# Two of the eight heads of the second group's convolution on GpSimd, in an eight-head convolution and token/channel mixer

## The chip, the cores and the metric

The kernel runs on one core of one Trainium2 chip. The metric is the device time of one execution in microseconds (us); of the kernel before there are three runs, and their median counts. "PE" is TensorE's matmul row in the profile, "PEld" its weight loads, "DVE" VectorE, "ACT" ScalarE, "POOL" GpSimd, "SP" the engine that only issues DMAs here.

## The reference

The input `x` has 8 batches of 4096 tokens with 192 channels. A causal convolution of 7 taps runs over the tokens, with one set of softmax weights for each of 8 heads of 24 channels. Its result `x` goes through a mix over the tokens and a mix over the channels, each two products with a maximum between them, added to what went in.

```python
w = softmax(weight, axis=-1)                       # 8 heads x 7 taps
x_unf = x_pad[:, idx, :].reshape(B, S, K, H, group)
x = np.einsum('hk,bskhg->bshg', w, x_unf)          # the convolution
xt = x.transpose(0, 2, 1)
h = np.maximum(xt @ w_tok1, 0.0) @ w_tok2          # token mix, 4096 -> 256 -> 4096
u = x + h.transpose(0, 2, 1)
h2 = np.maximum(u @ w_ch1, 0.0) @ w_ch2            # channel mix, 192 -> 1536 -> 192
return (u + h2).astype(np.float32)
```

## The kernel before

**Groups.** The batches are worked in five groups: batch 0, batch 1, then three pairs. For each group a *first stage* makes the convolution and the first token product (`stage1`, sums in `ps_a`, result `h1`). Then the group goes tile by tile (8 tiles of 512 tokens a batch) through the second token product (`mix2`), the transposes (`transposed`, result `own`), the first channel product (`channel1`, results `hh` and `hl`) and the second (`channel2`, result `osb`), and is stored. Products that need more than TensorE's reduced fp32 are split in a high and a low part: `hh`/`hl`, `own[0]`/`own[1]`, `t2s` and so on. ScalarE copies the high part out of PSUM (L973, L896), VectorE forms the low part as the difference (L974, L897).

**What runs beside what.** The first stage of group i+1 is worked in the background of the tiles of group i. For this change the stretch that matters is group 0's tiles, behind which three things run: the decoding of `w_tok2` (VectorE lines L172, L173, L176, L179 and L186 on 128x512 pieces, into `t2s`), the storing of its decoded pieces (ScalarE L1111 into `stage`, then a DMA of SP's queue), and the first stage of group 1, which is batch 1 alone (`nb == 1`). Groups 2 to 4 have two batches (`nb == 2`), and group 0's convolution is made on TensorE.

**The convolution of group 1.** It goes in four rounds (`q2` = 0 to 3) of 1024 tokens. For each round two halves of the input are loaded (`raw0` with heads 0 to 3, `raw1` with heads 4 to 7, one buffer each), with 8 tokens and 6 more of halo in each of 128 partitions. For each head, tap 0 is a scaled copy on ScalarE (L631) into the result `xc`, and taps 1 to 6 are six `scalar_tensor_tensor` instructions on VectorE (L633) that add weight times `raw` to `xc`, in place, on 128x192 elements. Heads go in pairs (`taps` runs heads h and h+1), so a call is two instructions of one tap. When a round is done, `store` sends `xc` to DRAM by a DMA of GpSimd's queue (L657), and 16 small matmuls per round (L721) add the round to `ps_a`. `xc` has two buffers in turn (`xc0`, `xc1`).

**The planner.** `Background` holds the background work as streams of items, each with a cost in VectorE's time. After each piece of a tile, `fg` adds that piece's TensorE and VectorE time to two running sums, and `fill` then takes items for as long as VectorE's sum is behind TensorE's (`if self.dve >= self.pe + until`). So the program order of all engines is set when the kernel is built, from these costs, and every engine works its own list in that order. A tap's item costs `2 * (RB * nb * G / 0.96 + 130)` ns, 660 for group 1. Among the streams the one goes first that has done the smallest share of its own total.

**GpSimd before** makes some set-up, two copies `u<-xc` of 128x768 (L912), small memsets (L623) and issues the stores `out_dram<-osb` (L1020) and `xcd<-xc` (L657) in program order, each waiting for its data at the head of the queue.

Of the kernel before, what the change touches and what calls it, by code (L numbers as in the profile page):

```python
# [8 lines left out]
F32 = mybir.dt.float32  # L9
# [3 lines left out]
ALU = mybir.AluOpType  # L13
# [101 lines left out]
def conv_mixer_kernel(ctx: ExitStack, tc: tile.TileContext, x, weight, w_tok1, w_tok2, w_ch1, w_ch2, out):  # L115
    nc = tc.nc
    B, S, D = x.shape
    H, K = weight.shape
    G = D // H
    JT = w_tok1.shape[1]  # L120
    FF = w_ch1.shape[1]
    P = 128
# [11 lines left out]
    RB = 8  # L134
# [20 lines left out]
    cw = const.tile([P, H, K], F32, name="cw")  # L155
# [442 lines left out]
    def stage1(gi, pools):  # L598
        bs = GROUPS[gi]
        nb = len(bs)  # L600
# [9 lines left out]
        HH, DH = H // 2, D // 2  # L610

        def load(q2, part):
# [10 lines left out]
                    nc.gpsimd.memset(raw[0:1, 0:HALO, i, :], 0.0)  # L623
            return raw

        def conv(raw, xc, h, k):
            rawm = raw.rearrange("p r b d -> p (r b) d")
            src = rawm[:, k * nb:(k + RB) * nb, h % HH * G:(h % HH + 1) * G]
            dst = xc[:, :, h * G:(h + 1) * G]
            if k == 0:  # L630
                nc.scalar.activation(out=dst, in_=src, func=AF.Copy, scale=cw[:, h, 0:1])  # L631
            else:
                nc.vector.scalar_tensor_tensor(  # L633
                    out=dst, in0=src, scalar=cw[:, h, k:k + 1], in1=dst, op0=ALU.mult, op1=ALU.add
                )
# [4 lines left out]
        def mark(*key):  # L640
            done[key] = max(bg.pe, bg.dve)

        def begin(q2, part):
            states[q2]["raw", part] = load(q2, part)
            mark("load", q2, part)

        def taps(q2, h, k):
            st = states[q2]
            if k == 0 and h == 0:
                st["xc"] = pools(q2 % 2).tile([P, RB * nb, D], F32, name=f"xc{q2 % 2}")  # L650
            for i in range(2):
                conv(st["raw", h // HH], st["xc"], h + i, k)

        def store(q2):
            xc = states[q2]["xc"].rearrange("p (j b) d -> p j b d", b=nb)
# [76 lines left out]
        def loaded(q2, part):  # L732
            at = done.get(("load", q2, part))
            return None if at is None or pools(q2 % 2) is None else at + (2e3 + 2e3 * nb if q2 else 10e3)

        def tap(q2, h, k):
            it = Item(lambda: taps(q2, h, k), cost=2 * (RB * nb * G / 0.96 + 130) if k else 0)
            if h % HH == 0 and k == 0:
                it.lag = 100

                def gate():
                    if h == 0 and q2 > 1 and ("split" if nb > 1 else "mixed", q2 - 2, last_q) not in done:
                        return None
                    return loaded(q2, h // HH)

                it.gate = gate
            convolving.append(it)
# [33 lines left out]
        for q2 in range(NS):  # L781

            tap(q2, 0, 0)
            for h in range(0, H, 2):
                for k in range(1, K):
                    if k == K // 2 and (h + 2) % HH:
                        tap(q2, h + 2, 0)
                    tap(q2, h, k)
                if h + 2 == HH:
                    tap(q2, HH, 0)  # L790
                if h % HH == HH - 2 and q2 + 1 < NS:
                    convolving.append(Item(lambda q2=q2, h=h: begin(q2 + 1, h // HH), lag=600))
            convolving.append(Item(lambda q2=q2: store(q2)))
            for q in range(0, last_q + 1, 2):

                for k in range(2):
                    prepare(q2, q + k)
                for k in range(2):
                    multiply(q2, q + k)
# [260 lines left out]
    def first_items():  # L1060
# [31 lines left out]
        def through():  # L1092

            decode_ctx.close()
            conv_pool(0)
            starts[2] = stage1(2, lambda k: cps[k])
# [28 lines left out]
    for gi, bs in enumerate(GROUPS):  # L1125
        nb = len(bs)
# [12 lines left out]
        for q in range(NT):  # L1139
            nxt = (gi, q + 1) if q + 1 < NT else (gi + 1, 0)  # L1140
            for i, b in enumerate(bs):
# [12 lines left out]
                if ahead:  # L1154
                    h = channel1(abc[i])
# [67 lines left out]
```

## Time and profile before

| | |
|---|---|
| median of 3 runs | 2064.75 us (2064.7 to 2065.62) |
| profiled execution, its own time | 2066.69 us |
| its span in the trace | 2064.8 us, granted TensorE clock 0.999 |
| busy: PE, PEld | 2052.5 us (99%), 1902.8 us (92%) |
| busy: DVE, ACT, POOL | 1404.0 us (68%), 760.2 us (37%), 101.7 us (5%) |
| chain that ended last | PE 90%, DVE 6%, DMA 2%, ACT 1% |

A line such as `L633 DVE ... x192 | 68.4, 412` gives a group of instructions: 192 of them were busy 68.4 us together, 412 ns each; instructions of one engine overlap at their ends, so that the sum over a group can be less than count times mean, and the distance between two starts ("pitch") is less than a duration. In the timeline a row has the start and the length of a run of like instructions and, in brackets, how long the engine had been idle before it and for whom. In a table of windows each engine has its busy time and its count of instructions.

### The profile page before, as it was taken

How to read it: one execution, taken by the hardware profiler on the slowest of the kernel's cores; microseconds unless marked ns; L12 is line 12 of the kernel's file. 1: busy time of each engine (PE TensorE's matmuls, PEld its weight loads, DVE VectorE, ACT ScalarE, POOL GpSimd, SP SyncE). 2: the span in 40 equal slices, each digit the busy share in tenths (PEclk: the TensorE clock that was granted, in tenths of full speed). 3: DMA queues.
4: the chain of work that ended last, by engine and by line, in shares of the span. 5: the costliest groups of instructions: out<-in, count | busy, mean ns of one | idle time of the engine just before them, and what ended most of it. 6: DMA issues, size and time to landing. Idle time of an engine off the chain costs nothing.

```text
span 2064.8 us, 41285 instructions
## 1 busy us (share of the span) xinstructions
PE 2052.5 (99%) x17723; PEld 1902.8 (92%) x17723; DVE 1404.0 (68%) x2781; ACT 760.2 (37%) x1305; POOL 101.7 (5%) x167
## 2 busy tenths in 40 slices
PE   9999999999999999999999999999999999999999
PEld 9889999998989989999999999999999999999998
DVE  8899979999559988448965778444445444444444
ACT  4656544434333333224323433233223232233222
POOL 0100000000000000000000000000000000000000
PEclk9999999999999999999999999999999999999999
DMA  9855436554354564232543433322211212222210
GB/s 308 291 154 183 138 120 197 180 164 137 132 160 136 177 170 132 78 103 74 151 124 90 129 122 108 98 60 67 67 45 52 65 50 67 59 67 67 67 32 17
DMA packets 259654, 239.44 MB, mean 116 GB/s; under 512 B 202832, under 2 KB 213584, under 8 KB 257936
## 3 DMA queue, kind: packets, MB, share of 16 engines
q1 hardware_dynamic: 243616, 158.55, 26.6%
q0 software_dynamic: 15856, 78.26, 11.8%
q8 instruction: 140, 2.29, 0.4%
q14 instruction: 42, 0.34, 0.1%
HBM read 146.60 MB, written 71.30 MB: 106 GB/s over the span
## 4 chain that ended last, share of the span: by engine, by line
PE 90%; DVE 6%; DMA 2%; ACT 1%; issue 1%; SPq 0%; POOL 0%; ACTq 0%; POOLq 0%
PE ps_x L934 35%; PE ps_x L1008 16%; PE ps_x L991 16%; PE ps_x L1009 7%; DVE xc L633 2%; PE ps_x L894 2%; PE ps_x L864 2%; PE ps_a L725 2%; PE ps_x L866 2%; PE ps_a L726 2%; PE ps_a L727 2%; PE ps_x L865 2%; DVE hl L974 1%; PE ps_a L426 1%; DMA t2d<-stage 1%; DMA dec_raw<-in_moe_w_tok_dram 1%
## 5 line engine op out<-in xcount | busy, mean ns | idle before, releaser
L973 ACT ACTIVATE hh<-ps_x 128x512 fp32r<-128x512 f32 x756 | 411.1, 597 | 807.2 <-PE ps_x L934 807.1
L974 DVE SCALAR_TENSOR_TENSOR hl<-ps_x,hh 128x512 fp32r<-128x512 f32 x756 | 485.1, 685 | 218.2 <-ACT hh L973 217.7
L934 PE MATMUL ps_x<-own,w_hi 64*128 64x512 f32 x2880 | 607.6, 390 | 1.4 <-DVE hl L974 1.2
L1008 PE MATMUL ps_x<-w,hh 128*128 128x384 f32 x1872 | 542.6, 361 | 0.7 <-DVE hl L974 0.6
L934 PEld LDWEIGHTS ps_x<-own,w_hi 64*128 64x128 f32 x2880 | 429.4, 184 | 55.9 <-issue 6.5
L1009 PE MATMUL ps_x<-w,hl 128*128 128x192 f32 x1872 | 468.8, 250 | 0.0
L934 PE MATMUL ps_x<-other,w_hi 64*128 64x512 f32 x1728 | 450.9, 389 | 0.5 <-DVE osb L1013 0.3
L633 DVE SCALAR_TENSOR_TENSOR xc<-raw,cw,xc 128x384 f32<-128x384 f32 (+1 forms) x768 | 388.7, 561 | 9.2 <-ACT xc L631 9.2
L1009 PEld LDWEIGHTS ps_x<-w,hl 128*128 128x128 f32 x1872 | 357.5, 191 | 0.0
L1008 PEld LDWEIGHTS ps_x<-w,hh 128*128 128x128 f32 x1872 | 351.4, 188 | 1.5 <-DVE hl L974 1.5
L934 PEld LDWEIGHTS ps_x<-other,w_hi 64*128 64x128 f32 x1728 | 314.0, 184 | 33.9 <-DVE hl L974 1.8
L991 PE MATMUL ps_x<-w,hh 64*128 64x384 f32 x2304 | 329.9, 355 | 0.0
L934 PE MATMUL ps_x<-own,w_lo 64*128 64x512 f32 x1440 | 326.5, 387 | 0.0
L991 PE MATMUL ps_x<-w,hl 64*128 64x192 f32 x2304 | 292.2, 247 | 0.1
L934 PE MATMUL ps_x<-other,w_lo 64*128 64x512 f32 x864 | 242.1, 386 | 0.0
L934 PEld LDWEIGHTS ps_x<-own,w_lo 64*128 64x128 f32 x1440 | 218.1, 184 | 24.4
L991 PEld LDWEIGHTS ps_x<-w,hl 64*128 64x128 f32 x2304 | 223.4, 188 | 1.7 <-DVE hl L974 0.8
L991 PEld LDWEIGHTS ps_x<-w,hh 64*128 64x128 f32 x2304 | 219.5, 184 | 0.9
L1012 DVE TENSOR_TENSOR osb<-ps_x,u 128x192 f32<-128x192 f32 x156 | 55.4, 355 | 205.1 <-PE ps_x L1009 204.9
L934 PEld LDWEIGHTS ps_x<-other,w_lo 64*128 64x128 f32 x864 | 159.0, 184 | 16.7
L896 ACT CAST own<-ps_x 128x512 fp32r<-128x512 f32 x120 | 63.4, 595 | 268.7 <-PE ps_x L894 268.5
L999 DVE TENSOR_TENSOR osb<-ps_x,osb 128x192 f32<-128x192 f32 x288 | 103.0, 358 | 17.0 <-DVE osb L999 0.5
(135 smaller groups left out, 1880.4 us busy)
## 6 DMA issues: line engine op xcount, KB each, us to landing
raw<-in_x_dram SPq DMA_DIRECT2D x56, 672.0 KB, 7.4
t<-t2d SPq DMA_DIRECT2D x64, 512.0 KB, 5.0
out_dram<-osb POOLq DMA_DIRECT2D x63, 384.0 KB, 4.3
u<-xcd SPq DMA_DIRECT2D x62, 384.0 KB, 5.6
xcd<-xc POOLq DMA_DIRECT2D x28, 768.0 KB, 7.4
other<-own POOLq DMA_DIRECT2D x24, 768.0 KB, 5.4
t<-t1p SPq DMA_DIRECT2D x32, 512.0 KB, 4.1
t2d<-stage SPq DMA_DIRECT2D x16, 512.0 KB, 4.3
```

Source lines behind the costliest of these rows:

```text
L633: nc.vector.scalar_tensor_tensor(out=dst, in0=src, scalar=cw[:, h, k:k + 1], in1=dst, op0=ALU.mult, op1=ALU.add)
L725: nc.tensor.matmul(out=ps, lhsT=wh, rhs=xh, start=a, stop=False)
L726: nc.tensor.matmul(out=ps, lhsT=wh, rhs=xl, start=False, stop=False)
L896: nc.scalar.copy(out=own[:, 0, c], in_=ps)
L934: nc.tensor.matmul(out=ps, lhsT=w1[w][rows, c, p * P:(p + 1) * P], rhs=t[h][rows, v, c], start=n == 0, stop=n == len(prods) - 1,)
L973: nc.scalar.activation(out=h["hh", f], in_=ps, func=AF.Relu)
L974: nc.vector.scalar_tensor_tensor(out=h["hl", f], in0=ps, scalar=0.0, in1=f32(h["hh", f]), op0=ALU.max, op1=ALU.subtract)
L991: nc.tensor.matmul(out=ps[:, :m], lhsT=h[part, f][ks, ts], rhs=w2[ks, f, :m], start=n == 0 and part == "hh", stop=z and part == "hl",)
L999: nc.vector.tensor_tensor(out=osb[:, j], in0=v, in1=osb[:, j], op=ALU.add)
L1008: nc.tensor.matmul(out=ps[:, :2 * D], lhsT=h["hh", f][:, ts], rhs=w2[:, f, :], start=n == 0, stop=False)
L1009: nc.tensor.matmul(out=ps[:, :D], lhsT=h["hl", f][:, ts], rhs=w2[:, f, :D], start=False, stop=z)
L1012: nc.vector.tensor_tensor(out=rows(osb[:, j]), in0=rows(ps[:, :D]), in1=tokens(u, i)[:, j], op=ALU.add)
```

## The change

A new function `conv_aside` forms a whole head on GpSimd: for tap 0 a `tensor_scalar` product straight into `xc`, and for each of the taps 1 to 6 a product into a small tile `prod` (128x192) and a `tensor_tensor` sum of `prod` and `xc` into `xc`: 13 instructions for a head. It is used where `nb == 1`, which is group 1, for heads 3 and 7 (`h % HH == HH - 1`), all of it at the place in the program where tap 0 of that pair was. VectorE's and ScalarE's instructions of these heads are gone: in four rounds 48 on VectorE and 8 on ScalarE, and 104 are added on GpSimd. The planner's cost of a tap of such a pair is halved.

```diff
+        def conv_aside(pool, raw, xc, h):
+            dst = xc[:, :, h * G:(h + 1) * G]
+            prod = pool.tile([P, RB, G], F32, name="prod")
+            for k in range(K):
+                src = raw[:, k:k + RB, 0, h % HH * G:(h % HH + 1) * G]
+                nc.gpsimd.tensor_scalar(
+                    out=prod if k else dst, in0=src, scalar1=cw[:, h, k:k + 1], scalar2=None, op0=ALU.mult
+                )
+                if k:
+                    nc.gpsimd.tensor_tensor(out=dst, in0=prod, in1=dst, op=ALU.add)
+
+        def aside(h):
+            return nb == 1 and h % HH == HH - 1
+
         def taps(q2, h, k):
...
             for i in range(2):
-                conv(st["raw", h // HH], st["xc"], h + i, k)
+                if not aside(h + i):
+                    conv(st["raw", h // HH], st["xc"], h + i, k)
+                elif k == 0:
+                    conv_aside(pools(q2 % 2), st["raw", h // HH], st["xc"], h + i)
...
-            it = Item(lambda: taps(q2, h, k), cost=2 * (RB * nb * G / 0.96 + 130) if k else 0)
+            it = Item(lambda: taps(q2, h, k), cost=(2 - aside(h + 1)) * (RB * nb * G / 0.96 + 130) if k else 0)
```

**On GpSimd**, from the two memsets of `raw` on: the order of the program before and of the changed one. `osb` is a finished tile of group 0, `xc_897` and the next `xc` are rounds 0 and 1 of the convolution, `raw_765` and `raw_768` the two halves of round 0's input.

```order
L623 MEMSET raw_765 1x576
L623 MEMSET raw_768 1x576
L1020 DMA out_dram<-osb 128x4x192 x2
L657 DMA xcd_76<-xc_897 128x1536
L1020 DMA out_dram<-osb 128x4x192
L657 DMA xcd_76<-xc_1507 128x1536
```

```order
L1038 DMA out_dram<-osb 128x4x192
L631 TENSOR_SCALAR xc_897<-raw_765,cw 128x8x24
L631 TENSOR_SCALAR prod<-raw_765,cw 128x192
L635 TENSOR_TENSOR xc_897<-prod,xc_897 128x8x24
...
L631 TENSOR_SCALAR xc_897<-raw_768,cw 128x8x24
...
L1038 DMA out_dram<-osb 128x4x192
L675 DMA xcd_76<-xc_897 128x1536
L631 TENSOR_SCALAR xc_1439<-raw_1211,cw 128x8x24
```

Between two stores of `xc` there stands now one block of 26 instructions, the 13 of head 3 and the 13 of head 7 of one round, and it stands behind the store of the round before and the store of a tile. (Lines behind the new function are higher by up to 18: L633 is L644 now, L974 is L992, L1020 is L1038.)

**On VectorE**, at the first channel product of the second of the tiles that have convolution behind them (`hl` are the low parts that it gives, `dec_top` and `t2s` the decoding): before, round 0 is still being finished there; now round 1 is.

```order
L974 SCALAR_TENSOR_TENSOR hl_1321<-ps_x,hh_1320 128x512 x2
L172 TENSOR_SCALAR dec_top<-dec_top 128x512
L974 SCALAR_TENSOR_TENSOR hl_1321<-ps_x,hh_1320 128x512 x2
L186 TENSOR_TENSOR t2s<-dec_top,t2s 128x512
L974 SCALAR_TENSOR_TENSOR hl_1323<-ps_x,hh_1322 128x512 x2
L633 SCALAR_TENSOR_TENSOR xc_897<-raw_768,cw,xc_897 128x8x24 x2
L974 SCALAR_TENSOR_TENSOR hl_1323<-ps_x,hh_1322 128x512 x2
L633 SCALAR_TENSOR_TENSOR xc_897<-raw_768,cw,xc_897 128x8x24 x2
```

```order
L992 SCALAR_TENSOR_TENSOR hl_1350<-ps_x,hh_1349 128x512 x2
L179 SCALAR_TENSOR_TENSOR dec_top<-dec_raw,dec_top 128x512
L992 SCALAR_TENSOR_TENSOR hl_1350<-ps_x,hh_1349 128x512 x2
L644 SCALAR_TENSOR_TENSOR xc_1439<-raw_1211,cw,xc_1439 128x8x24 x2
L992 SCALAR_TENSOR_TENSOR hl_1352<-ps_x,hh_1351 128x512 x2
L644 SCALAR_TENSOR_TENSOR xc_1439<-raw_1211,cw,xc_1439 128x8x24 x2
L992 SCALAR_TENSOR_TENSOR hl_1352<-ps_x,hh_1351 128x512 x2
L644 SCALAR_TENSOR_TENSOR xc_1439<-raw_1211,cw,xc_1439 128x8x24 x4
```

The room between the same pairs of `hl` is filled as densely as before, with work that used to come later. Counted in the two orders, from the first `hl` of one tile to the first of the next:

| tile | taps (L633) and decoding steps before | after |
|---|---|---|
| T1 | 34 and 10 | 26 and 14 |
| T2 | 42 and 14 | 36 and 16 |
| T3 | 42 and 14 | 36 and 15 |
| T4 | 46 and 12 | 36 and 6 |
| T5 | 18 and 1 | none, and 24 taps of group 2 |
| T6 | 24 taps of group 2 | none |

On TensorE the last 16 small matmuls of the convolution's rounds (L721) were all in T5; 8 of them are in T4 now and 8 in T5.

## The prediction

> **What bounds the kernel now.** I read the page first. TensorE has a matmul in flight for 99% of the span, VectorE is busy for 68%, and VectorE's load lies in the first fifth of the slices:
>
> ```profile
> PE 2052.5 (99%) x17723; PEld 1902.8 (92%) x17723; DVE 1404.0 (68%) x2781; ACT 760.2 (37%) x1305; POOL 101.7 (5%) x167
> DVE  8899979999559988448965778444445444444444
> ```
>
> So the kernel runs at TensorE's pace, and VectorE can matter only where it is full too. The change touches group 1's convolution. The view of the tile `raw` up to 260 us (count, shortest/median/longest in ns, first and last start) puts its taps behind tiles T1 to T5 of group 0:
>
> ```profile
> L633 DVE SCALAR_TENSOR_TENSOR xc<-raw,cw,xc x189: 406/411/421, 99.9 to 259.7; 128x192 f32<-128x192 f32 x189
> ```
>
> I therefore asked for the table of windows with one window for each tile, from the first channel product (L934) of one to that of the next: T1 to T5, and T6 for comparison. The columns are window, length, then busy time and count of PE, PEld, DVE, ACT, POOL, the granted clock and the DMA share:
>
> ```profile
> 99.62:131.73 32.11, 31.16 (x234) 28.26 (x234) 31.53 (x79) 21.22 (x38) 0.75 (x1) 1.00 0.45 145
> 131.73:167.03 35.30, 35.30 (x265) 33.47 (x264) 34.62 (x87) 22.78 (x39) 1.31 (x2) 1.00 0.65 196
> 167.03:202.93 35.90, 35.88 (x265) 32.72 (x265) 35.59 (x90) 19.85 (x37) 1.31 (x2) 1.00 0.50 147
> 202.93:240.06 37.13, 35.84 (x267) 34.25 (x266) 35.26 (x89) 19.14 (x36) 1.31 (x2) 1.00 0.57 184
> 240.06:275.21 35.15, 35.15 (x267) 33.75 (x266) 25.04 (x62) 19.25 (x30) 1.88 (x3) 1.00 0.45 144
> 275.21:305.13 29.92, 29.92 (x234) 28.85 (x234) 26.61 (x55) 11.87 (x25) 1.28 (x2) 1.00 0.20 63
> ```
>
> T6 and T5 show TensorE's own pace with VectorE slack (26.61 of 29.92, 25.04 of 35.15): 29.92 us for a tile without the convolution's matmuls (L721), 35.15 with 16 of them, so 5.23 for the 16. T1 has none, T2 to T4 have 16 each. Against that pace T1 is 2.19 us long, T2 0.15, T3 0.75, T4 1.98: together 5.07 us, 0.25% of the kernel. In T1 to T3 VectorE is idle for only 0.58, 0.68 and 0.31 us. So **VectorE and TensorE are level there**: taking work from VectorE can win 5 us at the very most, and each microsecond put on it beyond a small room is paid in full. TensorE's waits between 95 and 245 us name VectorE (total, times, longest):
>
> ```profile
> PE ps_x L934 <- DVE hl L974: 0.8, 1, 0.8
> PEld ps_x L934 <- DVE hl L974: 2.0, 3, 1.3
> ```
>
> A difference of 0.2%, 4.1 us, is about what a measurement of this kernel can tell from none.
>
> **What VectorE is relieved of.** A tap's pitch is read from a run of four and the next row (first column start, second length):
>
> ```profile
> 120.68 1.39 DVE L633 SCALAR_TENSOR_TENSOR xc<-raw,cw,xc 128x192 f32<-128x192 f32 x4
> 122.00 0.68 DVE L179 SCALAR_TENSOR_TENSOR dec_top<-dec_raw,dec_top 128x512 uint32<-128x512 uint32 x1
> ```
>
> 1.32 us for four is 0.33 each, and 48 of them are 15.8 us. ScalarE loses eight first taps; it is busy for 21 of 32 us in T1 and I count that at nothing. But the planner knows that the taps got cheaper and fills the room again. With the counts of the two orders (a tap 0.33, a decoding step 0.5 us on average by the rows below) VectorE's list becomes shorter by 0.7 us in T1 (8 taps less, 4 steps more), 1.0 in T2, 1.5 in T3, 6.3 in T4; the remaining 6.4 us are in T5, which already had 10 us idle. So where VectorE is the limit only 3.2 of the 15.8 us arrive.
>
> **What GpSimd's instructions take.** No row shows a product or a sum on GpSimd. The nearest are two memsets, which read nothing, and a copy with one input:
>
> ```profile
> L397 POOL MEMSET corner<- 128x1024 f32 x1 | 0.9, 946 | 0.0
> L408 POOL MEMSET x<- 128x192 f32 x1 | 0.3, 253 | 0.0
> 24.04 0.82 POOL L912 COPY u<-xc 128x768 f32<-128x768 f32 x1 [19.74 <-ACT xc L505]
> ```
>
> The memsets give (946 - 253) / 832 = 0.83 ns an element. The copy is then 0.64 us of elements and 0.18 fixed, and a product on 192 elements 0.16 + 0.18 = 0.34 us; its bounds are 0.25 (the memset of this size) and 0.82 (the copy of four times the size). A sum reads two streams: 0.32 + 0.18 = 0.50 if they take turns, with 0.34 and again 0.82 as bounds. I take 0.34 and 0.50, the scaled copy being the nearest kind. A block of two heads is 14 x 0.34 + 12 x 0.50 = 10.8 us, the four are 43 us, on an engine that was busy for less than 2 us in each tile above. By itself that hides.
>
> The Trainium skill, "GPSIMD Engine Reference", section "3.1 Elementwise — side-by-side cycle accounting", gives about 2.6 cycles an element at 1.2 GHz for a two-input operation, and its section 4.1 advises VectorE for elementwise work for this reason; an estimate from it is 0.42 us of elements for 192, so 0.60 with the fixed 0.18; the four blocks would be 48 us, a tenth more than mine, and the sum at the end +7 instead of +6.
>
> **What they cost VectorE.** GpSimd's two copies are the only rows where it reads SBUF beside a busy VectorE, and both show a blockade. The first rows are the first copy's neighbour and the same instruction undisturbed, then the second copy, its two neighbours, and the like of the last undisturbed:
>
> ```profile
> 24.09 1.32 DVE L172 TENSOR_SCALAR t<-t 128x1024 f32<-128x1024 f32 x1
> 20.48 0.69 DVE L172 TENSOR_SCALAR t<-t 128x1024 f32<-128x1024 f32 x1 [1.24 <-ACT t L170]
> 57.14 1.33 POOL L912 COPY u<-xc 128x768 f32<-128x768 f32 x1 [32.28 <-PE ps_x L859]
> 57.71 0.35 DVE L871 TENSOR_TENSOR u<-ps_x,u 128x192 f32<-128x192 f32 x1
> 57.97 1.31 DVE L176 SCALAR_TENSOR_TENSOR dec_top<-dec_raw,dec_top 128x768 uint32<-128x768 uint32 x1
> 71.86 0.96 DVE L176 SCALAR_TENSOR_TENSOR w2f<-dec_raw,w2f 128x768 uint32<-128x768 uint32 x1
> ```
>
> The L172 issued at 24.09, inside the copy of 24.04 to 24.86, took 1.32 instead of 0.69 us: it ended at 25.41, so it began in effect at 24.72, 0.14 us before the copy's recorded end. The second copy took 1.33 instead of 0.82, behind a VectorE instruction already running, and L176 at 57.97 took 1.31 instead of 0.96. The L871 between them, which reads PSUM and one SBUF tile, took its usual 0.35. So an instruction with two SBUF inputs, or the `tensor_scalar` L172, does not run at the same time as GpSimd's reading ones; one with a PSUM input does. The tap L633 reads `raw` and `xc`, both in SBUF: it is of the blocked kind. The Trainium skill, "SBUF — State Buffer", section "Who interferes with whom", states this as an exclusive lock on a port pair that VectorE's two-port modes and two-SBUF-input operations share with GpSimd, whoever starts first holding it to its end; the trace agrees (0.69 became 1.32), and it speaks against this change.
>
> How much of VectorE's time is of that kind is read from its groups between 95 and 275 us and the window's total:
>
> ```profile
> 95.00:275.00 180.00, 177.74 (x1317) 166.77 (x1316) 165.44 (x409) 104.32 (x181) 6.39 (x10) 1.00 0.52 164
> L633 DVE SCALAR_TENSOR_TENSOR xc<-raw,cw,xc 128x192 f32<-128x192 f32 x192 | 68.4, 412 | 1.0 <-ACT xc L631 1.0
> L974 DVE SCALAR_TENSOR_TENSOR hl<-ps_x,hh 128x512 fp32r<-128x512 f32 x60 | 38.5, 683 | 1.6 <-ACT hh L973 1.4
> L176 DVE SCALAR_TENSOR_TENSOR dec_top<-dec_raw,dec_top 128x512 uint32<-128x512 uint32 x12 | 8.3, 688 | 0.2
> L179 DVE SCALAR_TENSOR_TENSOR dec_top<-dec_raw,dec_top 128x512 uint32<-128x512 uint32 x12 | 8.2, 684 | 0.0
> L186 DVE TENSOR_TENSOR t2s<-dec_top,t2s 128x512 fp32r<-128x512 f32 x12 | 8.2, 684 | 0.0
> L173 DVE TENSOR_SCALAR dec_top<-dec_top 128x512 uint32<-128x512 uint32 x12 | 5.1, 427 | 0.0
> L172 DVE TENSOR_SCALAR dec_top<-dec_top 128x512 f32<-128x512 f32 x12 | 5.0, 419 | 0.4 <-ACT dec_top L170 0.4
> ```
>
> Decoding is 34.8 us in 60 steps, 0.58 each by duration and some 0.5 by pitch (the L179 further up lasts 0.68 and is 0.60 ahead of its follower). After the change the taps are 68.4 x 144/192 = 51.3, so blocked kinds are 86 of 165.4 - 17.1 = 148 us, 58%. GpSimd's blocks start behind a tile's store, so at a first channel product, where `hl` (PSUM input) takes more than half of VectorE's time; I take 50%. The share of GpSimd's 43 us, less 0.14 for each of 104 instructions at their end, is 0.5 x (43 - 15) = 14 us; where both engines have the next instruction ready they take turns, which puts more of GpSimd's work beside blocked kinds, up to 0.5 x 43 = 22. I take **18 us, 4.5 a block**. Bounds: all 104 at 0.25 give 0.5 x 104 x 0.11 = 6 us (1.5 a block), nothing if it never meets; products 0.5 and sums 0.82 give 0.5 x 67 = 34 us (8.5 a block).
>
> **The sum.** T1 to T3 have one block each: VectorE's list grows by 4.5 - 0.7 = 3.8, 3.5 and 3.0 us, together 10.3. From it go the 1.6 us in which VectorE was idle there, and 2 us of lag that six PSUM buffers let pass (an estimate: the planner counts 2.04 us of L934 to fill a pair, and the longest wait of 1.3 above says that there is hardly more). TensorE pays 6.7. T4 has 35.26 - 6.3 + 4.5 = 33.5 us of VectorE work against 35.15 + 2.6 of TensorE's, since half of T5's small matmuls move into it; VectorE is no limit there any more. T4 and T5 were 72.28 and are 70.3 at TensorE's pace. Of the 2.0 us between, 1.3 was a hole whose chain goes back to the DMA of `stage`, which may stay:
>
> ```profile
> 201.89 12.46 DMA t2d<-stage x2
> 210.00:220.00 10.00, 8.71 (x69) 7.75 (x66) 8.44 (x18) 7.68 (x13) 0.00 (x0) 1.00 0.66 231
> ```
>
> I count -1.0. The net is +5.7. The profiled execution takes 2066.69 with a span of 2064.8; the runs' median is 2064.75, and a difference made on the span goes onto that: **2070.5 us**. Later groups have the same items (group 2's first taps move one tile up, into T5's free room), and TensorE at its pace: nothing.
>
> **Rivals.** *It relieves* (0.24): GpSimd's instructions mostly meet `hl` and other PSUM readers, or hold their inputs far more briefly than recorded, so VectorE nets a gain. Against it are both copies, each with a blockade; for it, the blocks' place at the first channel product. At 1.5 us a block T1 to T3 come to -3.2 + 4.5, about their old pace, and T4 and T5 give 1 to 2 back: 2063; with no blockade at all T1 to T3 lose up to 3 of their 3.1 us, so 2060.5. *GpSimd's sums are slow* (0.14): at 1 us for a sum and 0.6 for a product a block is 20.4 us, half of it blocks, 10 a block; T1 to T3 pay 30 - 3.2 - 3.6 = 23.2, T4's list of 39.0 us exceeds TensorE's 37.8 by 1.2 and T4 and T5 together then give back 0.8: 2087. From 8.8 us a block on T4 is short too. *GpSimd is late* (0.04): round n's small matmuls wait for its heads. A block starts when the last round's store is issued; the stores stand some 41 us apart:
>
> ```profile
> 144.16 0.55 POOL L657 DMA_DIRECT2D xcd<-xc  x1 [8.86 <-DVE xc L633]
> 184.61 0.55 POOL L657 DMA_DIRECT2D xcd<-xc  x1 [13.17 <-DVE u L876]
> ```
>
> So a block of 26 must exceed 1.5 us an instruction to be late; at 1.65 it is 3 us late, in four rounds 12 us, 2077. That the planner's new order doesn't relieve VectorE (the change not doing what it says) is already in the sum.
>
> **How the numbers follow.** My case, blocking of 3 to 8 us a block (0.58), runs from about +1 (3 x 3 - 3.2 - 3.6 = +2.2, less 1.0) to +16 (24 - 3.2 - 3.6, less 1.0). Of it I put 0.20 within 4.1 us and 0.38 above; of the relieving case 0.16 within and 0.08 faster; both other rivals are slower. Sums: faster 0.08, same 0.36, slower 0.56. The range 2061.5 to 2083 leaves out the best of the relieving case and the slow sums.
>
> **What would show it.** In the profile after: L644 with a mean above 412 ns and a maximum near 0.9 us, in the four blocks only, L992 unchanged at 683; GpSimd busy by some 60 us more (its own waits for VectorE count in its durations); T1 to T3 longer by some 2 us each, T4 and T5 together not; waits of L934's matmuls for `hl` of 5 us or more. It is wrong if taps beside GpSimd keep 412 ns, if T1 to T3 shorten, or if L739's matmuls wait for GpSimd.

## The result, and the profile after

The change makes the kernel slower: 2079.09 us, the median of 6 runs (2078.08 to 2081.08), against 2065.02 us (2063.58 to 2065.9) for the kernel before, also 6 runs. That is a ratio of 1.0069, with a 95% interval of 1.0059 to 1.0079, or 14.1 us. The forecast was 2070.5 us, in a range of 2061.5 to 2083.0.

The page of the profile after, whose own execution took 2079.59 us, has a span of 2077.8 us, 13.0 more than before:

```profile
span 2077.8 us, 41331 instructions
PE 2057.4 (99%) x17723; PEld 1897.6 (91%) x17723; DVE 1401.9 (67%) x2733; ACT 756.4 (36%) x1297; POOL 180.6 (9%) x271
```

VectorE has 48 instructions less and yet is busy for nearly as long: 1401.9 us against 1404.0, where the 48 taps were worth 15.8. The table of windows by tile, T1 to T5, in the columns of the prediction's table:

```profile
99.92:132.57 32.65, 31.43 (x233) 27.84 (x232) 32.30 (x72) 20.20 (x35) 20.49 (x27) 1.00 0.44 142
132.57:170.34 37.77, 36.62 (x265) 33.10 (x265) 35.38 (x81) 23.16 (x39) 21.63 (x28) 1.00 0.65 204
170.34:211.45 41.11, 38.27 (x265) 34.45 (x264) 38.54 (x86) 22.78 (x40) 20.67 (x28) 0.96 0.56 165
211.45:255.78 44.33, 40.04 (x281) 35.59 (x281) 39.11 (x90) 20.75 (x36) 21.44 (x30) 1.00 0.41 144
255.78:288.26 32.48, 32.48 (x250) 31.21 (x249) 23.37 (x47) 13.48 (x25) 1.75 (x3) 1.00 0.33 100
```

The lengths were 32.11, 35.30, 35.90, 37.13 and 35.15 us, together 175.59; they are 188.34 now. So 12.8 of the span's 13.0 us are in these five tiles, and T3 and T4 have most of it. (The two profiled executions are 12.9 us apart and the medians 14.1, since that of before was 1.7 us above its runs' median and that of after 0.5.) The trace counts 32 small matmuls in each of T2 to T5 before, 16 for each of the two sums `ps_a`, where the part ahead and the prediction say 16; the 5.23 us are the price of all 32. T4 has 48 of them now and T5 has 16, so their own pace is 37.77 and 32.5. T4 is thus 6.6 us over its pace, T3 6.0, T5 not at all. VectorE is idle for only 0.35 us in T1, but for 2.4, 2.6 and 5.2 us in T2 to T4: it is late, and it still waits.

The groups of GpSimd between 60 and 330 us give what its instructions take:

```profile
L631 POOL TENSOR_SCALAR prod<-raw,cw 128x192 f32<-128x192 f32 x48 | 41.8, 871 | 3.9
L635 POOL TENSOR_TENSOR xc<-prod,xc 128x192 f32<-128x192 f32 x48 | 30.7, 640 | 4.0
L631 POOL TENSOR_SCALAR xc<-raw,cw 128x192 f32<-128x192 f32 x8 | 6.2, 777 | 0.1
```

A product takes 0.87 us on average, a sum 0.64; the four blocks are 78.7 us, not 43. The groups of VectorE in the five tiles show what that does to it:

```profile
L644 DVE SCALAR_TENSOR_TENSOR xc<-raw,cw,xc 128x192 f32<-128x192 f32 x144 | 61.9, 465 | 5.4 <-ACT xc L642 4.6
L992 DVE SCALAR_TENSOR_TENSOR hl<-ps_x,hh 128x512 fp32r<-128x512 f32 x60 | 38.4, 679 | 9.6 <-ACT hh L991 9.6
L176 DVE SCALAR_TENSOR_TENSOR dec_top<-dec_raw,dec_top 128x512 uint32<-128x512 uint32 x12 | 9.0, 752 | 0.1
L186 DVE TENSOR_TENSOR t2s<-dec_top,t2s 128x512 fp32r<-128x512 f32 x12 | 8.9, 742 | 0.0
L173 DVE TENSOR_SCALAR dec_top<-dec_top 128x512 uint32<-128x512 uint32 x12 | 6.1, 509 | 0.0
L172 DVE TENSOR_SCALAR dec_top<-dec_top 128x512 f32<-128x512 f32 x12 | 5.4, 447 | 0.0
```

A tap has gone from 412 to 465 ns, the decoding steps from 688, 684, 427 and 419 to 752, 742, 509 and 447; `hl`, which reads PSUM and one SBUF tile, is at 679 (683 before), and the step L179 at 685 (684 before). Multiplied out, (465 - 412) x 144 and the four differences times 12 are 7.6 + 2.8 = **10.4 us of blockade, 2.6 a block**. The rows of `hl` and of the taps end with a second change: 9.6 and 5.4 us of idle time before them, in which VectorE waits mostly for ScalarE. Of the 9.6 us for `hl` 7.2 lie in T5, where VectorE has time to spare. In T1 to T4 these waits are 2.4 us for `hl` and 4.6 for the taps, where before they were 1.4 and 1.0.

One place in the timeline shows the blockade itself (first column start, second length; x2 is a run of two):

```profile
112.85 1.27 DVE L992 SCALAR_TENSOR_TENSOR hl<-ps_x,hh 128x512 fp32r<-128x512 f32 x2
113.21 0.61 POOL L635 TENSOR_TENSOR xc<-prod,xc 128x192 f32<-128x192 f32 x1
121.99 1.23 DVE L644 SCALAR_TENSOR_TENSOR xc<-raw,cw,xc 128x192 f32<-128x192 f32 x2
122.40 0.60 POOL L635 TENSOR_TENSOR xc<-prod,xc 128x192 f32<-128x192 f32 x1
124.20 0.60 POOL L635 TENSOR_TENSOR xc<-prod,xc 128x192 f32<-128x192 f32 x1
124.23 0.84 DVE L173 TENSOR_SCALAR dec_top<-dec_top 128x512 uint32<-128x512 uint32 x1
```

Two `hl` beside the sum of 113.21 take what two of them always take. The two taps that the sum of 122.40 runs into take 1.23 instead of 0.74 us, and the L173 that starts just behind the start of the sum of 124.20 takes 0.84 instead of 0.43.

TensorE's waits between 95 and 290 us, then the start of T3 and of T4 and the end of T4 in TensorE's and VectorE's timeline (in brackets the idle time before):

```profile
PE ps_x L952 <- DVE osb L1031: 3.9, 2, 2.7
PE ps_x L952 <- DVE hl L992: 2.3, 3, 1.0
PE ps_a L739 <- issue: 2.0, 1, 2.0
...
177.68 0.92 PE L952 MATMUL ps_x<-own,w_hi 64*128 64x512 f32 x5 [2.73 <-DVE osb L1031]
180.04 1.29 DVE L992 SCALAR_TENSOR_TENSOR hl<-ps_x,hh 128x512 fp32r<-128x512 f32 x2 [1.18 <-ACT hh L991]
219.55 1.29 DVE L992 SCALAR_TENSOR_TENSOR hl<-ps_x,hh 128x512 fp32r<-128x512 f32 x2 [1.18 <-ACT hh L991]
220.30 1.56 PE L952 MATMUL ps_x<-own,w_hi 64*128 64x512 f32 x6 [0.82 <-DVE hl L992]
250.91 0.86 DVE L644 SCALAR_TENSOR_TENSOR xc<-raw,cw,xc 128x192 f32<-128x192 f32 x2
251.87 1.54 PE L739 MATMUL ps_a<-xc,t 128*128 128x192 f32 x8 [2.02 <-issue]
```

VectorE's last `osb` of the tile before, which reads `ps_x` and so frees a PSUM bank, is so late that the new tile's first product (L952) stops in the middle for 2.73 us; `hh` of that product is then late, and VectorE, late itself, waits 1.18 us for it. At the start of T4 the same happens in small. Such a wait on both sides gives back nothing of VectorE's lag. The third wait, 2.02 us in T4, has no releaser in its row. It stands before small matmuls of the last round, half of which the new order has moved into T4. The last two taps of that round end at 251.77 us, 0.1 us before TensorE goes on, while GpSimd's last sum was done at 240.0. So here too TensorE waited for a late VectorE, and without GpSimd's work (first experiment below) this wait does not appear.

### The profile page after: what moved, and what is told of

Its sections match the earlier page's. It is cut to its first block, busy times and chain, and to the rows that moved or that the text cites. A ratio compares the mean times of both kernels' runs of the same rounds, so it can differ in the third digit from the quotient of the medians.

```text
span 2077.8 us, 41331 instructions
## 1 busy us (share of the span) xinstructions
PE 2057.4 (99%) x17723; PEld 1897.6 (91%) x17723; DVE 1401.9 (67%) x2733; ACT 756.4 (36%) x1297; POOL 180.6 (9%) x271
## 4 chain that ended last, share of the span: by engine, by line
PE 89%; DVE 7%; DMA 1%; ACT 1%; issue 1%; SPq 0%; ACTq 0%
PE ps_x L952 35%; PE ps_x L1026 16%; PE ps_x L1009 16%; PE ps_x L1027 7%; DVE xc L644 3%; PE ps_x L912 2%; PE ps_x L882 2%; PE ps_a L743 2%; PE ps_x L884 2%; PE ps_a L744 2%; PE ps_a L745 2%; PE ps_x L883 2%; DVE hl L992 1%; PE ps_a L426 1%; PE ps_x L879 1%; DMA dec_raw<-in_moe_w_ch_dram 1%
## 5 line engine op out<-in xcount | busy, mean ns | idle before, releaser
L992 DVE SCALAR_TENSOR_TENSOR hl<-ps_x,hh 128x512 fp32r<-128x512 f32 x756 | 484.9, 685 | 226.4 <-ACT hh L991 226.1
L952 PE MATMUL ps_x<-own,w_hi 64*128 64x512 f32 x2880 | 613.7, 391 | 7.4 <-DVE osb L1031 3.9
L952 PEld LDWEIGHTS ps_x<-own,w_hi 64*128 64x128 f32 x2880 | 428.0, 185 | 70.2 <-issue 11.3
L952 PE MATMUL ps_x<-other,w_hi 64*128 64x512 f32 x1728 | 451.0, 389 | 0.5 <-DVE osb L1031 0.3
L644 DVE SCALAR_TENSOR_TENSOR xc<-raw,cw,xc 128x384 f32<-128x384 f32 (+1 forms) x720 | 381.9, 582 | 14.4 <-ACT xc L642 13.7
L952 PEld LDWEIGHTS ps_x<-other,w_hi 64*128 64x128 f32 x1728 | 314.0, 184 | 33.5 <-DVE hl L992 1.8
L952 PE MATMUL ps_x<-own,w_lo 64*128 64x512 f32 x1440 | 327.4, 387 | 0.0
L952 PE MATMUL ps_x<-other,w_lo 64*128 64x512 f32 x864 | 242.1, 386 | 0.0
L952 PEld LDWEIGHTS ps_x<-own,w_lo 64*128 64x128 f32 x1440 | 217.2, 184 | 26.1
L952 PEld LDWEIGHTS ps_x<-other,w_lo 64*128 64x128 f32 x864 | 159.0, 184 | 16.6
L1038 POOL DMA_DIRECT2D out_dram<-osb x63 | 37.1, 588 | 901.6 <-DVE osb L1017 618.1
```

Of the source, the lines that this page charges most:

```text
L644: nc.vector.scalar_tensor_tensor(out=dst, in0=src, scalar=cw[:, h, k:k + 1], in1=dst, op0=ALU.mult, op1=ALU.add)
L952: nc.tensor.matmul(out=ps, lhsT=w1[w][rows, c, p * P:(p + 1) * P], rhs=t[h][rows, v, c], start=n == 0, stop=n == len(prods) - 1,)
L992: nc.vector.scalar_tensor_tensor(out=h["hl", f], in0=ps, scalar=0.0, in1=f32(h["hh", f]), op0=ALU.max, op1=ALU.subtract)
```

## The experiments

The theory was the prediction's with one more term: VectorE is held up where GpSimd reads SBUF, and the planner has filled the relief with other work in advance, so that TensorE pays. What had to be told apart: the new order by itself, GpSimd's work by itself, which part of that work, and whether single taps or the refilling make the order dear. All times are medians; differences are to the kernel before on the same chip (2065.01, 2064.87 and 2065.15 us in the three sets). A ratio of "this to before" has its 95% interval.

**The new order without GpSimd's work, and with writes only.** In the first, each block is one memset a head; in the second, 33 memsets a head, nearly as long as the work but without a read.

```diff
 def conv_aside(pool, raw, xc, h):
-    prod = pool.tile([P, RB, G], F32, name="prod")
-    for k in range(K):
...
+    nc.gpsimd.memset(xc[:, :, h * G:(h + 1) * G], 0.0)
```

The second has, besides:

```diff
+    fill = pool.tile([P, RB, G], F32, name="prod")
+    for _ in range(2 + 5 * (K - 1)):
+        nc.gpsimd.memset(fill, 0.0)
```

> GpSimd only writes zeros into heads 3 and 7 of the second group (one memset a head, 8 in all, which leaves out these heads' convolution); the lists of VectorE, ScalarE and TensorE are those of the changed kernel. Theory A (GpSimd's reading instructions block VectorE by some 2.9 us a block, and TensorE pays since the planner has filled the freed room): without them 2060 to 2065 us, no slower than before. Theory B (the new order is at fault: taps of one head in a row, decoding earlier, small matmuls earlier): most of the loss stays, 2071 to 2079 us.

> The changed kernel with GpSimd's 13 instructions of a head replaced by 33 memsets of 128x192 that read nothing, some 8 us a head as before (the convolution of heads 3 and 7 is left out). Theory A in its narrow form (only GpSimd instructions that read SBUF block VectorE's reading of two SBUF tiles): taps keep 412 ns and the time is that without the work, 2060 to 2066 us. Rival D (a busy GpSimd blocks as such, by writes too): 2073 to 2081 us, taps again near 465 ns.

Measured: 2068.9 us (+3.9; 1.0020, 1.0011 to 1.0029) and 2068.76 us (+3.75; 1.0020, 1.0011 to 1.0029). The groups of VectorE and GpSimd in the second:

```profile
L640 DVE SCALAR_TENSOR_TENSOR xc<-raw,cw,xc 128x192 f32<-128x192 f32 x144 | 54.1, 413 | 5.4 <-ACT xc L638 4.7
L631 POOL MEMSET prod<- 128x192 f32 x256 | 68.9, 269 | 14.3
```

GpSimd is busy for 69 us beside the taps, and these keep 413 ns, as theory A of the second run had it (its range of times lies 2.8 us too low). So memsets, which read nothing, do not hold VectorE up, products and sums do, and what these cost in the changed kernel is 2079.1 - 2068.9 = 10.2 us. But 3.9 us are lost without any of it: the new order is slower than the old one although 48 taps are gone, and neither theory of the first run had this time. The tiles T3 and T4 of the first kernel, VectorE's waits for ScalarE in T2 (one row) and T3 (two rows), and one place in T2:

```profile
167.00:205.71 38.71, 36.78 (x266) 33.04 (x265) 36.03 (x89) 23.80 (x40) 1.76 (x4) 1.00 0.64 194
205.71:244.89 39.18, 38.88 (x281) 35.29 (x281) 33.99 (x84) 19.65 (x34) 2.48 (x6) 1.00 0.42 144
...
DVE xc L636 <- ACT xc L634: 1.9, 1, 1.9
DVE hl L984 <- ACT hh L983: 1.2, 1, 1.2
DVE xc L636 <- ACT xc L634: 0.9, 1, 0.9
...
156.01 0.35 ACT L888 COPY u<-u 128x192 f32<-128x192 f32 x1 [1.08 <-DVE u L887]
156.27 1.18 ACT L1121 CAST stage<-t2s 128x512 fp32r<-128x512 f32 x1
157.36 0.80 ACT L634 ACTIVATE xc<-raw,cw 128x192 f32<-128x192 f32 x2
157.84 0.77 DVE L636 SCALAR_TENSOR_TENSOR xc<-raw,cw,xc 128x192 f32<-128x192 f32 x2 [1.87 <-ACT xc L634]
```

VectorE stands still for 1.87 us because its next tap needs ScalarE's first tap, and that stands in ScalarE's order behind a copy that had waited 1.08 us for VectorE and a cast of 1.18. The plan has no cost for ScalarE; that filling it up brings such places closer together is my reading and not shown.

The lists were counted ahead of the prediction from the first `hl` of one tile to that of the next. Divided at these places, the table of windows gives length and, in brackets, VectorE's busy time in us:

| from `hl` to `hl` | before | the order alone | with GpSimd's work |
|---|---|---|---|
| T1 | 30.37 (30.09) | 30.61 (30.05) | 32.83 (32.27) |
| T2 | 35.48 (34.80) | 38.22 (34.65) | 40.65 (37.11) |
| T3 | 35.01 (34.70) | 36.56 (33.95) | 39.51 (36.90) |
| T4 | 37.49 (35.62) | 36.37 (29.53) | 39.21 (32.44) |

With the order alone VectorE's list in T1 to T3 is shorter by only 0.9 us, partly since a single tap behind another of its own head starts later: a run of three took 1.32 us at 170.11, where one of four took 1.39 before. Its idle time there rises from 1.3 to 6.7 us, and 5.2 of these are waits for ScalarE: the three above and one more of 1.2 us for `hh` at the start of T4. GpSimd's work then adds 2.2 to 2.9 us of busy time to each of the four stretches, 10.6 in all.

**The old order with and without the work.** The planner is told the old cost of a tap; the instructions are those of the change (first) or one memset a head (second).

```diff
-cost=(2 - aside(h + 1)) * (RB * nb * G / 0.96 + 130)
+cost=2 * (RB * nb * G / 0.96 + 130)
```

> The change as it is, but the planner goes on charging 660 ns for a tap of a pair of which GpSimd has one head, so that VectorE's list has a hole of 0.33 us at each of 48 places, 15.8 us against 13.4 us of measured delay. Theory A: the loss goes, 2063 to 2068 us. Theory C (what GpSimd blocks is lost whatever room the list has, since the holes lie elsewhere than the blocks): 2074 us or more.

> The planner counts heads 3 and 7 as before (so the order stays that of before, and VectorE's 48 taps are simply missing from it), and GpSimd writes one memset a head in place of the 13 products and sums; heads 3 and 7 are left out of the result. It is the ceiling of what the change could give. Theory A (TensorE's time over its own pace in T1 to T5 is VectorE's lag, and it was only the planner's refilling that stopped the missing taps from paying): the 5.07 us over pace mostly go, 2060.5 to 2062.5 us, T1 to T5 at 30 to 31, 35.2, 35.2, 35.2 to 36 and 35.2 us. Theory B (VectorE's total load in these stages was no limit of before; the excess over pace is made by short waits in a row, for ScalarE's copies, for PSUM banks and at the start of a tile, which 15.8 us less of VectorE's work leave as they are): 2064 to 2065.5 us, not to be told from before.

Measured: with the work 2065.84 us (+0.8; 1.0006, 0.9997 to 1.0015), as theory A had it; without it 2063.0 us (-1.9; 0.9993, 0.9984 to 1.0002), between the ranges of its two theories. The tiles T2 to T4 without the work:

```profile
130.97:166.07 35.10, 35.10 (x266) 32.49 (x265) 32.35 (x77) 22.95 (x38) 1.76 (x4) 1.00 0.68 213
166.07:201.20 35.13, 35.13 (x267) 32.48 (x266) 32.28 (x77) 19.40 (x35) 1.58 (x3) 1.00 0.50 154
201.20:236.33 35.13, 35.13 (x266) 34.02 (x266) 32.08 (x77) 18.55 (x34) 1.84 (x4) 1.00 0.56 175
```

TensorE is at its own pace of 35.1 us in each, and VectorE has 3 us left. T1 alone stays 1.4 us above. So 1.9 us is about all that taking these taps off VectorE could have given, less than a measurement of this kernel can tell. The four cases together:

| difference to before, us | no work | GpSimd's work |
|---|---|---|
| planner's old cost | -1.9 | +0.8 |
| planner's new cost | +3.9 | +14.1 |

The same work costs 2.7 us where the freed slots stay empty (the intervals of these two overlap, so it may be less) and 10.2 where they are filled again. With the old cost VectorE is held up no less: the taps' mean is 486 ns there.

```profile
L644 DVE SCALAR_TENSOR_TENSOR xc<-raw,cw,xc 128x192 f32<-128x192 f32 x144 | 64.7, 486 | 1.6 <-ACT xc L642 1.0
```

That is (486 - 412) x 144 = 10.7 us on the taps alone, and it fits into the 15.8 us that the missing taps leave.

**GpSimd's work added to the kernel before.** VectorE keeps all taps and the order is that of before; the 104 instructions go into a scratch tile that nobody uses (`prod` = `raw` times weight, `prod` = `prod` + `raw`), then the 56 products alone, then the 48 sums alone.

```diff
 for i in range(2):
     conv(st["raw", h // HH], st["xc"], h + i, k)
+    if nb == 1 and k == 0 and (h + i) % HH == HH - 1:
+        conv_aside(pools(q2 % 2), st["raw", h // HH], h + i)
```

> The kernel before with all its taps on VectorE, and GpSimd's 104 instructions added, which read the same input and leave their sums in the small buffer, unused. Theory A: VectorE's list is as full as before and gets some 12 us of blockade, 2075 to 2082 us. Theory B (order): no order changed, 2064 to 2068 us.

> Before, whole, with only GpSimd's 56 products added, into a scratch tile that nobody reads. Products and sums together added 12.2 to 12.7 us. Theory A (a VectorE instruction waits long only where a sum stands beside it or hands over to a product; beside a product alone it waits 0.09 us): 2067 to 2069.5 us, with products at 0.75 to 0.8 us. Theory B (each reading instruction of GpSimd costs alike): 56 of 104 of 12.5 us, 2071 to 2072.5 us.

> Before, whole, with only GpSimd's 48 sums added, on a scratch tile and the raw rows. Theory A (the sums, which read two operands, make the waits): most of the 12.5 us, 2071 to 2075 us. Theory B (each reading instruction costs alike): 48 of 104 of 12.5 us, 2070 to 2071.5 us. If the two runs of products and of sums alone add up to much less than 12.5 us, the waits come from the two alternating on GpSimd, and neither theory holds.

Measured: both 2077.72 us (+12.7; 1.0064, 1.0052 to 1.0077), products 2067.12 us (+2.25; 1.0011, 1.0002 to 1.0020), sums 2073.43 us (+8.6; 1.0042, 1.0029 to 1.0055). Taps and GpSimd's groups of the products' run, then of the sums':

```profile
L641 DVE SCALAR_TENSOR_TENSOR xc<-raw,cw,xc 128x192 f32<-128x192 f32 x192 | 70.2, 420 | 1.0 <-ACT xc L639 1.0
L630 POOL TENSOR_SCALAR prod<-raw,cw 128x192 f32<-128x192 f32 x56 | 52.4, 935 | 5.8 <-DMA raw<-in_x_dram 1.0
```

```profile
L640 DVE SCALAR_TENSOR_TENSOR xc<-raw,cw,xc 128x192 f32<-128x192 f32 x192 | 75.8, 450 | 1.0 <-ACT xc L638 1.0
L631 POOL TENSOR_TENSOR prod<-prod,raw 128x192 f32<-128x192 f32 x48 | 32.5, 677 | 6.2 <-DMA raw<-in_x_dram 2.5
```

Each of the three times lies in the range of its theory A. The products take more of GpSimd's time, 0.935 us each where 0.75 to 0.8 was expected, and cost little; the sums make four fifths of the 10.8 us that the two are together (12.7 in one kernel, whose trace has a stretch at half clock in T3, worth up to 1.6). Their 38 ns on 192 taps are 7.3 us and with the decoding steps 8.9: about the 8.6 us by which the kernel became slower. Worked out in the same way the products come to 2.2 us for 2.25 measured, and both together (taps at 461 ns) to 12.1 for 12.7. In the old and full order, then, a microsecond of VectorE's is a microsecond of the kernel's.

**Is it the single taps?** The order filled anew and no work, but with a whole pair, heads 4 and 5, left out in place of 3 and 7, so that no tap stands alone behind another that it depends on.

```diff
-return nb == 1 and h % HH == HH - 1
+return nb == 1 and h // 2 == 2
-cost=(2 - aside(h + 1)) * (...)
+cost=2 * (not aside(h)) * (...)
```

> As the run with the new order and one memset a head (heads left out of the result), but with heads 4 and 5, a whole pair, in place of 3 and 7, and the planner told that their taps cost nothing: the same 48 taps are refilled, and no tap stands alone behind another that it depends on. With the old cost and no work the time was 2063.0 us, with the new cost and no work 2068.9 us; the 5.9 us between are the price of the refilled order. Theory A (the single taps in a row, about 2.8 us longer than the planner's cost, are a large part of that price): 2064.5 to 2067 us. Theory B (the refilled order is dear by itself: ScalarE's first taps and the copies come late, and VectorE and TensorE wait for each other at the starts of T3 and T4): 2068 to 2070 us.

Measured: 2067.46 us (+2.3; 1.0013, 1.0004 to 1.0022), in the middle between the two ranges. Of the 5.8 us between -1.9 and +3.9 the single taps may be 1.6 and the refilling 4.2; heads 4 and 5 also stand elsewhere in the order than 3 and 7, so this division is rough. T3 and T4, with 37.03 and 40.17 us, are the long ones again. In T1 to T4 VectorE waits 2.4 us for `hh`, as with the single taps, and for first taps 2.2 us instead of 4.6; from `hl` to `hl` its list in T1 to T3 is shorter than before by 1.9 us instead of 0.9.

**The true cost.** The changed kernel with a pair charged at 1.72 taps, what it takes with the blockade.

```diff
-cost=(2 - aside(h + 1)) * (...)
+cost=(2 - 0.28 * aside(h + 1)) * (...)
```

> The change as it is, but the pair with a head on GpSimd is charged at 1.72 taps in place of 1 (1 for the tap that is left, 0.06 us for standing behind its like and 11.6 us over 48 slots for GpSimd's blockade, together 0.72 of 0.41 us). Theory A (the loss comes because the planner filled time that VectorE does not have; charged at what it takes, the slots hold): 2065.5 to 2068 us. Theory B (any refilling pays the waits at the starts of T3 and T4, and the blockade falls where it falls): 2070 to 2076 us, on the line from 2065.8 us at 2 taps to 2079.1 us at 1.

Measured: 2069.44 us (+4.3; 1.0021, 1.0012 to 1.0030). The first theory is missed by 1.4 us. The second said "on the line" between the times at 2 taps and at 1: that line is at 2065.8 + 0.28 x 13.3 = 2069.5, which is what came, though I had set the range from 2070. So the refilling was not free at this cost either; that each slot filled again costs as much as the one before fits this one point and is not shown further.

**Fewer heads, and other heads, at the old cost.** Head 7 alone (the diff shown); heads 0 and 1, by `h < 2`; heads 4 and 5, by `h // 2 == 2`. All three have the old cost's line from above.

```diff
-return nb == 1 and h % HH == HH - 1
+return nb == 1 and h == H - 1
```

> The change with the planner's old cost and head 7 alone on GpSimd (head 3 back on VectorE): half of the relief and half of the work. Between before (2064.9 to 2065.0 us) and the two heads at the old cost (2065.8 us). Theory A (relief and blockade grow alike with the number of heads, and both end in slots that TensorE does not wait for): 2064.5 to 2065.8 us, not to be told from before. Theory B (the relief pays first, up to the 1.9 us that the missing work gave, and the blockade of a half block is absorbed): 2063 to 2064.3 us.

> The change with the planner's cost of before and with heads 0 and 1, a whole pair of one half, put on GpSimd in place of heads 3 and 7: VectorE's taps then all come in pairs, none runs behind another that it depends on. Theory A (of the loss, the single taps in a row made 1 to 2 us, and the old order absorbs GpSimd's work as it did with heads 3 and 7, 2065.8 us): 2063.5 to 2065 us. Theory B (the blocks of two heads, 26 instructions in a row, now lie in one half of each tile, and VectorE's relief lies beside them where it is at the same time held up): 2065.5 to 2068 us.

> The change with the planner's old cost and heads 4 and 5, the first pair of the second half, on GpSimd. Heads 0 and 1 at the old cost took 2076.7 us, heads 3 and 7 2065.8 us. Theory A (the first pair lost because its block began at 90 us, where VectorE decodes weights that TensorE waits for, and again under the conversions at 117 and 224 us; a pair whose data come some 10 us later misses these): 2063.5 to 2066 us. Theory B (two heads of one half put all 26 instructions in one stretch and beside the same steps of VectorE, wherever it lies): 2070 to 2077 us.

Measured: one head 2066.59 us (+1.4; 1.0008, 0.9998 to 1.0017), first pair 2076.74 us (+11.9; 1.0059, 1.0046 to 1.0071), late pair 2071.77 us (+6.6; 1.0032, 1.0020 to 1.0045). One head cannot be told from before; its median is 0.8 us above theory A's range, and that relief pays first is refuted. The first pair is more than 8 us above both of its ranges. Its block begins at 90 us, in T0; T0, T1 and T4 took 41.5, 36.9 and 40.95 us for 36.2, 32.1 and 37.1 of before. TensorE's waits in T1 and T4, and its granted clock (eighth from the left in the window's row) in T0 and behind the wait in T1:

```profile
PE ps_x L879 <- DVE hl L992: 6.8, 2, 3.9
...
86.00:87.00 1.00, 0.32 (x1) 0.07 (x1) 1.00 (x1) 1.00 (x2) 0.00 (x0) 0.80 0.76 184
122.00:123.00 1.00, 1.00 (x6) 1.00 (x5) 0.62 (x2) 1.00 (x3) 0.00 (x0) 0.50 0.07 29
128.00:129.00 1.00, 1.00 (x9) 1.00 (x8) 1.00 (x4) 1.00 (x3) 0.00 (x0) 1.00 0.00 0
```

In T1 TensorE stops for 3.9 us, and behind that it runs at half clock for nearly 7: in one microsecond it starts 5 or 6 of the matmuls of which it later starts 9. In T0 the clock falls at 86 us, 4 us before the block begins, and stays at half for 10 us; so what T0 lost in this execution was not begun by the block. The late pair has neither of these waits; it has a new one, the third rival of the prediction, at T5:

```profile
PE ps_a L739 <- POOL xc L635: 2.9, 1, 2.9
...
240.80:282.07 41.27, 38.37 (x265) 35.41 (x265) 23.02 (x50) 19.31 (x30) 20.68 (x29) 0.92 0.38 123
```

TensorE waits 2.9 us for GpSimd's last sum, and T5 is 6.1 us over its pace, at a clock of 0.92 (0.08 of its 41.27 us are the other 3.3). Both pairs are worse than heads 3 and 7: the late one mainly because its block ends late; for the first I take it that its blocks lie beside steps that TensorE waits for next, but no run shows that apart. For the late pair the second theory gave the time, but not this cause. No run beats the kernel before; only that with the old cost and no work lies below it, and it leaves two heads out.

## Why the prediction was right, and where it was not

**The direction** was right and the size too small: +5.7 forecast, +14.1 measured, inside the range.

**GpSimd's durations** were too short. A product was put at 0.34 us; undisturbed ones take 0.755 to 0.777 in the trace. A sum was put at 0.50 and is 0.59 to 0.61. The blocks took 21 to 22 us each, from the first start to the last end, not 10.8. The length itself is hidden; the write-only run shows that 69 us of it cost nothing.

**The blockade** was forecast at 4.5 us a block, 18 in all; the groups show 2.6 and 10.4. The kinds were right (taps and decoding yes, `hl` no), but the share of a GpSimd instruction that blocks was not: I took all but 0.14 us of each, and a tap waited at most 0.18 us behind the start of a product and 0.38 behind that of a sum. The two errors pull against each other: with GpSimd's true 79 us the same working would have given 32 to 39 us of blockade. That the term came out less than double what it measured is luck.

**The room** of 3.6 us, idle time and buffers, which was to swallow part of it, did not exist: VectorE's idle time in T1 to T3 rose from 1.6 to 5.3 us. Together the errors cancel. Forecast for the work alone, against the same order without it, were 2070.5 - 2060.5 ("no blockade at all") = 10.0 us; measured are 10.2. This is luck as well, for nearly all of it was to fall in T1 to T3, with T4's block hidden, and by the two traces T1 to T3 took 5.4 us of it and T4 5.2.

**The step that failed** is the other one: that without a blockade "T1 to T3 lose up to 3 of their 3.1 us" and that in T4 "VectorE is no limit there any more", so that the order alone would give 2060.5 us. The run of exactly that case took 2068.9: the new order was counted at -4.2 us and is +3.9, which is 8.1 of the 8.4 us by which the forecast was too low. VectorE's list in T1 to T3 was counted 3.2 us shorter and is shorter by 0.9, and its idle time there, which I took for room, rose by 5.5 us, nearly all in waits for ScalarE. I compared sums of VectorE's and TensorE's time in a tile, and neither sum holds these waits; T3 alone took 38.71 us for 35.90 of before. In T4 I counted 33.5 us for VectorE against 37.75. From `hl` to `hl` its list there was busy 32.4 us with GpSimd's work, near what I counted; but it began 8.1 us behind TensorE's start of T4 (4.3 before), so the lag of the tiles before went into T4 and was paid there: in TensorE's T4 VectorE was busy for 39.11 us and idle for 5.2. T4 and T5 were to give 1.0 us back and took 4.5 instead (76.81 us for 72.28). T1 to T3 were forecast at +6.7 us and came to +8.2, of which the half clock behind the wait that ends at 177.68 is up to 1.6 (4% of T3's 41.11 us).

**The ceiling** of 5.07 us was too high as well. The old order with empty slots is at TensorE's pace in T2 to T5 and wins 1.9 us. The profile of before is of an execution 1.7 us above its runs' median, and what stands ahead of T1 and behind T5 is as long in it as in the run with empty slots (99.6 and 1789.6 us, there 99.6 and 1789.8): so the 1.7 us should lie in T1 to T5, and an ordinary execution was not 5.07 but some 3.4 us above TensorE's pace, 1.5 of them in T1, which stay.

**The signs** that were named came in part. The taps' mean is above 412 ns and `hl` keeps its time, but the longest tap took 0.80 us, not 0.9; GpSimd is busier by 79 us, not 60; T1 to T3 grew by 0.5, 2.5 and 5.2 us, not 2 each, and T4 and T5 together did grow; TensorE's first channel products waited 2.3 us for `hl` and 3.9 for `osb`.

**The rivals.** That the change relieves VectorE is refuted in both its forms: the taps are held up, and an unhindered relief is worth 1.9 us at the old cost and a loss at the new. Sums at 1 us did not come. GpSimd was not late in the changed kernel, but was in the run with the late pair.

What remains open: whether ScalarE's place in the order sets the +3.9 us of the order alone. The trace names the waits for it, but no run moved its first taps or casts, and the runs tell single taps from refilling only roughly.

## What to carry to other kernels

Where two engines run level, a cost in a planner is a change of its own: test a relief with the old cost first, and with the work left out, since that gives the ceiling before anything is built; here it was 1.9 us. Work given to GpSimd was not free for VectorE where both read SBUF, two-input sums above all, and the price went by which instructions met and how many, not by how long GpSimd was busy: 52 us of products cost 2.25 us, 33 us of sums 8.6. A sum of engine times per tile says whether an engine can be the limit; it does not say that a shorter list ends sooner.

## What the runs showed of the hardware

**How long a reading GpSimd instruction blocks.** The taps sorted by where they start within a GpSimd instruction (in the changed kernel's trace up to 253 us): in the first 0.2 us of a sum they took 335 to 370 ns longer (10 of them), between 0.3 and 0.4 us 110 ns longer (12), from 0.4 us on nothing (2). Behind an undisturbed sum, recorded with 0.60 us, the waiting taps got on some 0.40 us after its start, so its last third blocked no one: the lock to an instruction's end that the prediction quotes is not what these rows show. Behind the start of a product it is 176 ns at the most on average, and in its second half next to nothing (25 ns at most on average). The Trainium skill, "SBUF — State Buffer", section "Who interferes with whom", says that an instruction of VectorE with two SBUF inputs contends with GpSimd instructions that read, and not with those that only write. The traces agree: 465 and 450 ns beside reads, 413 beside memsets, and `hl`, with one SBUF input, 679 beside reads and 683 before.

**GpSimd suffers too.** An undisturbed product is 0.76 us; beside VectorE the mean is 0.87 to 0.94. Why it takes 0.76 us where a copy of four times the size took 0.82 was not tried.

**A short stop costs clock.** Behind the wait of 2.73 us at the start of T3 the changed kernel's trace has these rows:

```profile
178.00:179.00 1.00, 1.00 (x10) 0.98 (x8) 0.83 (x2) 0.10 (x1) 1.00 (x2) 0.83 0.35 82
179.00:180.00 1.00, 1.00 (x7) 0.96 (x7) 0.00 (x0) 1.00 (x3) 0.97 (x2) 0.50 1.14 259
182.00:183.00 1.00, 1.00 (x12) 0.84 (x10) 1.00 (x3) 1.00 (x4) 0.92 (x2) 0.97 1.10 388
```

About 1.0 us after TensorE has begun again at 177.68 the clock falls to half, and it stays there for some 3.4 us, worth up to 1.6 us. In the run with the first pair, waits of 3.9 and 2.9 us each come with nearly 7 us of it, begun before TensorE went on. The Trainium skill, "TensorE: Matmul & The Clock Gate", section "What's actually happening", puts the fall behind at least one idle window of about 3.4 us and the return behind a busy one as long. Here a wait of 2.7 us was enough for the fall, while the stretch of 3.4 us agrees. Not every execution has it: of the six runs of the changed kernel one shows a clock of 1.000 and a span of 2076.8 us, and two at 0.997 have 2076.3 and 2079.3. So the fall does not make the 14 us, and its share of them cannot be read from these runs.
